# Attention products in a fused attention and two-MLP kernel: three rounded products replaced by one fp32 product, with the two heads on separate parts of the array

## The chip, the cores and the metric

The kernel runs on 1 core of a Trainium2 chip. The metric is the device time of one execution, in microseconds (us). The kernel before takes 2152.38 us, the median of 3 runs (2146.97 to 2156.15). TensorE (PE in the profile) multiplies matrices, VectorE is DVE, ScalarE is ACT, GpSimd is POOL, and SyncE (SP) issues nearly all DMAs. PEld is the weight load of TensorE, which can lie beside the product before it.

## The reference

Three stages follow each other. Causal attention with a window of 128 and a linear position bias, for 4 batches, 8 heads, 576 positions and a head width of 64:

```
scores = q @ k.T / sqrt(64)
scores = where(0 <= rel < 128, scores - slope[h] * |rel|, -1e9)
attn   = softmax(scores)                 # sums get + 1e-9
x      = (attn @ v), heads side by side  # 2304 x 512, fp32
```

Then an MLP, `x = relu(x @ w_in)**2 @ w_out`, with w_in of 512 x 2048 and w_out of 2048 x 512. Then a soft mixture of 8 experts: gates from `x @ w_gate`, normalised 8 times over experts and tokens, and `sum over e of P[:, e] * (relu(x @ w1[e]) @ w2[e])`.

## The kernel before, in words

**Number formats.** TensorE takes two 32-bit formats here. In F32R a product is one pass, but its operands must have been rounded; to keep accuracy an operand is split into a rounded part (hi) and what is left (lo), and one product becomes three: hi·hi, hi·lo, lo·hi. The MLP and the experts are done in this way throughout (`mm3`, lines 119 to 121). In plain F32 nothing is split, and the trace shows each product as two PE instructions.

**Units of attention.** One unit is a batch, a pair of heads and either the first 384 query positions (three tiles of 128, here called a first unit) or the remaining 192 (a tile of 128 and one of 64; a rest unit). There are 32 units, 16 of each kind, in the order: the first units of batch 0 (4 pairs of heads), the rest units of batch 0, then batch 1, and so on. The two heads of a pair lie in the two halves of the partitions for q and k (64 rows each).

**Two ways of doing a unit.** The first `WHOLE_UNITS = 12` units (8 first units, 4 rest units) are done in plain F32: q is padded with zeros, so that a head's scores are a product over all 128 rows (lines 340 to 348), and the bias is added by a product with the identity. The other 20 units (8 first, 12 rest) are split: q, k, v and the softmax weights p each have a hi and a lo tile. Their scores (lines 352 to 354) are three products per head over that head's 64 rows; the bias is added on DVE (line 357).

**Values.** For all units, `block` (lines 396 to 410) multiplies v by the transposed weights. v lies with a block of 64 zero columns between its two heads, so that each head's product fills 128 columns and both heads add into the same 128 output partitions. A whole unit does one F32 product per head and block, a split unit three F32R products. A first unit does block 0 in the step of tile 1 and blocks 1 and 2 in the step of tile 2; a rest unit does blocks 3, 2 and 4 in one step (line 431).

**Where p and v come from.** p is transposed on TensorE into PSUM (line 392), copied by ACT (line 306 whole, line 114 split) and in a split unit subtracted by DVE (line 115). v of a whole unit is loaded straight into place when its scores are done (lines 279 to 285); v of a split unit is loaded with q and k two units ahead (line 205), then split by ACT and POOL (lines 290, 291).

**Order.** Attention is not a stage of its own. `plan` lists its steps (q: transpose q and k; s: scores; t: transpose p, then values), and `part` (called after parts of the MLP's steps) lets the attention steps of the next chunk of tokens run among the MLP products of the present one. Up to the start of the experts a scheduler orders the instructions of each engine; all that follows is in the order written. The attention products lie between 0 and 577 us of the span. PSUM banks of attention come from a pool of three (`ps_at`).

Of the kernel before, what the change touches and what calls it, by code (L numbers as in the profile page):

```python
# [29 lines left out]
def attention_moe_moe2(  # L30
# [12 lines left out]
    nc = tc.nc  # L43
# [125 lines left out]

    qtail, qwhole, vwhole, vsplit = [], [], [], []  # L170
    for i in range(SETS):

        qtail.append([ap.tile([P, 2, TAIL], F32R, name=f"qtail{i}{n}") for n in range(2)])
        qwhole.append(ap.tile([P, 7 * P], F32, name=f"qwhole{i}"))
        nc.gpsimd.memset(qwhole[i], 0.0)
        vwhole.append(ap.tile([P, 3, 3, D], F32, name=f"vwhole{i}"))
        nc.gpsimd.memset(vwhole[i][:, :, 1, :], 0.0)
        vsplit.append([ap.tile([P, 3, 3, D], F32R, name=f"vsplit{i}{n}") for n in range(2)])
        for n in range(2):
            nc.vector.tensor_scalar_mul(  # L180
                vsplit[i][n][:, :, 1, :], ones[:, None, :D].to_broadcast([P, 3, D]), 0.0
            )
    def tails_ready():

        for i in range(SETS):
            for n in range(2):
                nc.scalar.activation(qtail[i][n].rearrange("p j c -> p (j c)"), ones, AF.Copy, scale=0.0)
        for hp in range(NPAIR):
            for j in range(2):
                nc.scalar.copy(  # L190
                    tbias[j * TAIL : (j + 1) * TAIL, hp, :], raw(bias[0:TAIL, 2 * hp + j, : P + TAIL])
                )

    def attention_load(n, b, hp, rest):

        h0 = 2 * hp
        t = {"rest": rest, "alone": b == 0 and not rest, "whole": n < WHOLE_UNITS}
        for nm, src in (("k", k), ("q", q), ("v", v)):
            if nm == "v" and t["whole"]:
                continue  # L200
            r = t[nm] = ap.tile([P, 3, 2, D], F32, name=f"{nm}raw", tag=f"{nm}raw", bufs=2)
            r0 = 0 if not rest else EARLY - (0 if nm == "q" else P)
            r1 = FULL * P if rest else EARLY
            for j in range(2):
                nc.sync.dma_start(
                    r[:, : (r1 - r0) // P, j, :], src[b, h0 + j, r0:r1, :].rearrange("(t p) d -> p t d", p=P)
                )
            if rest:
                nc.sync.dma_start(
                    r[:TAIL, (r1 - r0) // P], src[b, h0 : h0 + 2, r1:, :].rearrange("j p d -> p j d")  # L210
                )
        return t

    def attention_qk(n, t):

        rest = t["rest"]
        hi, lo = {}, {}
        for nm in "k" if t["whole"] else "kq":
            hi[nm] = ap.tile([P, EARLY], F32R, name=f"{nm}h", tag=f"{nm}h", bufs=2)
            t[nm + "h"] = hi[nm]  # L220
            if not t["whole"]:
                lo[nm] = t[nm + "l"] = ap.tile([P, EARLY], F32R, name=f"{nm}l", tag=f"{nm}l", bufs=2)

        def put_whole(pk, pq):
            nc.scalar.copy(raw(hi["k"][:, : pk.shape[-1]]), pk)
            qw = t["qw"] = qwhole[n % SETS]
# [9 lines left out]
        def turn(ps, nm, blocks, tail):  # L236
# [7 lines left out]
            return ps[:, :o]  # L244

        if not rest:
            pk = turn(at_ps("tp_k", t), "k", 3, 0)
            if not t["whole"]:
                split_ps(pk, hi["k"], lo["k"])
            pq = turn(at_ps("tp_q", t), "q", 3, 0)  # L250
            if t["whole"]:
                put_whole(pk, pq)
            else:
                split_q(pq, hi["q"], lo["q"])
        else:
            both = at_ps("tp", t)
            w = 2 * P + TAIL
            pk = turn(both, "k", 2, 1)
            if not t["whole"]:
                split_ps(pk, hi["k"][:, :w], lo["k"][:, :w])  # L260
            pq = turn(both[:, w:], "q", 1, 1)
            if t["whole"]:
                put_whole(pk, pq)
                return
            split_q(pq[:, :P], hi["q"][:, :P], lo["q"][:, :P])
            t["qt"] = qtail[n % SETS]
            for j in range(2):
                r = slice(j * D, (j + 1) * D)
                split_q(pq[r, P:], *[x[r, j, :] for x in t["qt"]])

    def attention_v(n, t):

        rest = t["rest"]
        if t["whole"]:
            vh, = t["vs"] = [vwhole[n % SETS]]
            b, hp, _ = units[n]
            for j in range(2):
                src = v[b, 2 * hp + j]
                if rest:
                    nc.sync.dma_start(  # L280
                        vh[:, :2, 2 * j], src[2 * P : FULL * P].rearrange("(t p) d -> p t d", p=P)
                    )
                    nc.sync.dma_start(vh[:TAIL, 2, 2 * j], src[FULL * P :])
                else:
                    nc.sync.dma_start(vh[:, :, 2 * j], src[:EARLY].rearrange("(t p) d -> p t d", p=P))
            return
        vh, vl = t["vs"] = vsplit[n % SETS]
        cuts = [(slice(0, P), slice(0, 2)), (slice(0, TAIL), slice(2, 3))] if rest else [(slice(0, P), slice(0, 3))]
        for rows, ts in cuts:
            nc.scalar.activation(vh[rows, ts, ::2], t["v"][rows, ts], AF.Copy)  # L290
            nc.gpsimd.tensor_sub(vl[rows, ts, ::2], t["v"][rows, ts], raw(vh[rows, ts, ::2]))

    def split_q(ps, hi, lo):
        nc.scalar.activation(hi, ps, AF.Copy, scale=-(D ** -0.5))
        nc.vector.scalar_tensor_tensor(lo, ps, -(D ** -0.5), raw(hi), op0=ALU.mult, op1=ALU.subtract)

    def weights(t):
        return [
            ap.tile([P, 2, 6 * P], F32R, name=f"p{n}", tag=f"p{n}", bufs=2) for n in range(1 if t["whole"] else 2)
        ]  # L300

    def put_p(t, pv, rows, at):
        w = pv.shape[-1]
        dst = [x[:rows, :, at : at + w] for x in t["p"]]
        if t["whole"]:
            nc.scalar.copy(raw(dst[0]), pv)
        else:
            split_ps(pv, *dst)

    def attention_scores(hp, t, i):  # L310
# [16 lines left out]
        z = ap.tile([P, 2], F32, name="z", tag="z", bufs=3)  # L327
        ops = []
        for j in range(0 if t["whole"] else heads):
            r = slice(0, P) if tail else slice(j * D, (j + 1) * D)  # L330
            if tail:
                qh, ql = [x.rearrange("p j c -> p (j c)") for x in t["qt"]]
            else:
                qh, ql = [t[n][r, (i - qb0) * P : (i - qb0 + 1) * P] for n in ("qh", "ql")]
            kh, kl = [t[n][r, k0 : k0 + nk] for n in ("kh", "kl")]
            ops.append(((qh, kh), (qh, kl), (ql, kh)))
        if t["whole"]:
# [6 lines left out]
            for j, sc in enumerate(scs):  # L344
                q0 = 6 * P if tail else (2 * (i - qb0) + j) * P
                nc.tensor.matmul(
                    sc, lhsT=t["qw"][:, q0 : q0 + P], rhs=raw(t["kh"][:, k0 : k0 + nk]), start=False, stop=j == heads - 1,
                    skip_group_check=True,
                )
            nc.vector.tensor_reduce(out=m[:, :heads], in_=sv, op=ALU.min, axis=AX.X)  # L350
        else:
            for x in range(3):
                for sc, (lhs, rhs) in zip(scs, [o[x] for o in ops]):
                    nc.tensor.matmul(sc[:, :nk], lhsT=lhs, rhs=rhs, start=x == 0, stop=x == 2)  # L354
        for j, sc in enumerate(scs if not t["whole"] else ()):
# [18 lines left out]
    def attention_weights(t, i):  # L374
# [3 lines left out]
        if not t["p"]:  # L378
            t["p"] = weights(t)
        kb0 = 2 if t["rest"] else 0  # L380
        at = max(0, 2 * (i - kb0) - 1) * P
        pt = at_ps("pt", t)
        if tail:
            for kb in range(2):
                nc.tensor.transpose(pt[:, kb * P : (kb + 1) * P], s[:, 0, kb * P : (kb + 1) * P], ident)
            for kb, rows in ((0, P), (1, TAIL)):
                put_p(t, pt[:rows, kb * P : (kb + 1) * P].rearrange("p (j c) -> p j c", j=2), rows, at + kb * P)
            return
        pv = pt[:, : 2 * blocks * P].rearrange("p (j c) -> p j c", j=2)
        for j in range(2):  # L390
            for kb in range(blocks):
                nc.tensor.transpose(pv[:, j, kb * P : (kb + 1) * P], s[:, j, kb * P : (kb + 1) * P], ident)  # L392
        put_p(t, pv, P, at)

    def block(t, kb, dst, a, w, first, last):

        rows = TAIL if kb == FULL else P
        kb -= 2 if t["rest"] else 0
        vs = [x[:rows, kb].rearrange("p a d -> p (a d)") for x in t["vs"]]
        a += 2 * kb * P  # L400
        n, ops = 0, 1 if t["whole"] else 3
        for j in range(2):
            ls = [x[:, j * D : j * D + P] for x in vs]
            rs = [x[:rows, j, a : a + w] for x in t["p"]]
            for l, r in ((0, 0), (0, 1), (1, 0))[:ops]:
                l, r = (ls[0], raw(rs[0])) if t["whole"] else (ls[l], rs[r])
                nc.tensor.matmul(  # L407
                    dst, lhsT=l, rhs=r, start=first and n == 0, stop=last and n == 2 * ops - 1, skip_group_check=True
                )
                n += 1  # L410

# [925 lines left out]
```

## Time and profile before

| | |
|---|---|
| median of 3 runs | 2152.38 us |
| the profiled execution | 2151.79 us, span 2150.0 us |
| TensorE busy | 2087.5 us, 97% of the span |
| weight loads busy | 1915.1 us, 89% |
| DVE / ACT / POOL busy | 68% / 46% / 49% |
| granted TensorE clock, mean | 0.992 |
| the chain that ended last | PE 79%, DVE 10%, ACT 3%, DMA 3% |

A busy TensorE isn't one at its peak: the recorded length of a product holds its way through the array, and neighbours overlap. What a product costs is read from the distance of starts: from the start of a product before a group to the start of the second product behind it, less the usual distances of those products. The first product behind a group often starts by the record before its weights are there, so its own start isn't taken.

### The profile page before, as it was taken

What the parts mean: (1) busy time and instruction counts of PE and PEld (TensorE: products, weight loads), DVE (VectorE), ACT (ScalarE), POOL (GpSimd) and SP (SyncE); (2) the same over time, 40 slices, a digit from 0 to 9 for tenths busy, and PEclk for the clock granted to TensorE, in tenths of its full rate; (3) what the DMA queues carried; (4) which work ended last, traced back from release to release, by engine and by line L of the source; (5) the groups of instructions that cost most, each with busy time, mean ns of one, the idle gap of its engine ahead of it and who ended that gap; (6) DMA issues with size and microseconds to landing.
All of it is one profiled execution on the core that took longest, in us unless ns stands there. A gap on an engine that the chain in (4) does not pass through costs nothing.

```text
span 2150.0 us, 32105 instructions
## 1 busy us (share of the span) xinstructions
PE 2087.5 (97%) x11260; PEld 1915.1 (89%) x11260; DVE 1463.2 (68%) x2480; ACT 981.2 (46%) x1982; POOL 1054.7 (49%) x697
## 2 busy tenths in 40 slices
PE   6999999999999999999999999999999999999998
PEld 5887777777798788899998999999999999999998
DVE  7996444442425888887778567776678667777766
ACT  7775444443324444444444444444444444444343
POOL 1113223222246778888888445544447344554442
PEclk9999999999999999999999999999999999999999
DMA  7787546455574877798888977787877877778773
GB/s 211 233 248 243 154 135 176 134 157 167 199 243 168 313 272 289 281 333 293 309 300 305 333 261 255 249 271 260 258 259 266 267 257 257 258 244 275 260 260 125
DMA packets 281792, 525.46 MB, mean 244 GB/s; under 512 B 85648, under 2 KB 129824, under 8 KB 277536
## 3 DMA queue, kind: packets, MB, share of 16 engines
q1 hardware_dynamic: 281632, 523.42, 72.3%
q8 instruction: 90, 1.47, 0.3%
q14 instruction: 70, 0.57, 0.1%
HBM read 379.60 MB, written 143.73 MB: 243 GB/s over the span
## 4 chain that ended last, share of the span: by engine, by line
PE 79%; DVE 10%; ACT 3%; DMA 3%; issue 2%; POOL 1%; SPq 1%; ACTq 0%; POOLq 0%; DVEq 0%
PE y L120 9%; PE y L119 9%; PE y L121 9%; PE g L119 9%; PE g L121 9%; PE g L120 9%; PE xo L407 3%; PE h L119 3%; PE h L120 3%; PE h L121 3%; PE acc L119 3%; PE acc L121 3%; PE acc L120 2%; PE sc L354 1%; PE pt L392 1%
## 5 line engine op out<-in xcount | busy, mean ns | idle before, releaser
L1157 POOL TENSOR_TENSOR rb<-R,rb 128x768 fp32r<-128x768 f32 x95 | 210.8, 2220 | 337.6 <-ACT rb L1152 329.8
L1188 DVE TENSOR_TENSOR a<-y,a 128x384 f32<-128x384 f32 x434 | 239.8, 553 | 179.7 <-PE y L121 177.6
L1157 POOL TENSOR_TENSOR rt<-R,rt 128x768 fp32r<-128x768 f32 x125 | 238.9, 1923 | 146.4 <-issue 61.7
L111 POOL TENSOR_TENSOR gl<-r,gh 128x512 fp32r<-128x512 f32 (+1 forms) x80 | 99.3, 1242 | 403.9 <-ACT gh L110 388.9
L111 POOL TENSOR_TENSOR w2a<-r,w2a 128x1024 fp32r<-128x1024 f32 x64 | 155.0, 2422 | 66.7 <-ACT w2a L110 66.7
L1152 ACT ACTIVATE rt<-R 128x768 fp32r<-128x768 f32 x128 | 107.7, 842 | 148.0 <-DVE R L1139 89.6
L119 PE MATMUL g<-xt,w1o 128*128 128x384 f32 x512 | 172.9, 338 | 0.9 <-ACT u L880 0.6
L121 PE MATMUL g<-xt,w1o 128*128 128x384 f32 x512 | 172.5, 337 | 0.0
L119 PE MATMUL y<-rt,w2o 128*128 128x384 f32 x512 | 172.3, 336 | 0.2
L120 PE MATMUL g<-xt,w1o 128*128 128x384 f32 x512 | 172.3, 336 | 0.0
L121 PE MATMUL y<-rt,w2o 128*128 128x384 f32 x512 | 172.1, 336 | 0.0
L120 PE MATMUL y<-rt,w2o 128*128 128x384 f32 x512 | 171.8, 336 | 0.0
L119 PE MATMUL y<-w2a,rh 128*128 128x512 f32 x384 | 151.2, 394 | 0.0
L120 PE MATMUL y<-w2a,rh 128*128 128x512 f32 x384 | 150.8, 393 | 0.2 <-POOL w2a L111 0.2
L121 PE MATMUL y<-w2a,rl 128*128 128x512 f32 x384 | 150.1, 391 | 0.0
L1134 DVE TENSOR_TENSOR R<-R,pb 128x768 f32<-128x768 f32 x128 | 139.0, 1087 | 5.3 <-ACT R L1247 3.0
L769 DVE SCALAR_TENSOR_TENSOR r<-h,r 128x512 f32<-128x512 f32 (+1 forms) x80 | 50.9, 636 | 134.4 <-ACT r L767 134.3
L119 PE MATMUL y<-rb,w2o 128*128 128x384 f32 x384 | 130.3, 339 | 2.8 <-DVE a L1188 2.1
L120 PE MATMUL y<-rb,w2o 128*128 128x384 f32 x384 | 130.1, 339 | 2.4 <-POOL rb L1157 2.4
L121 PE MATMUL y<-rb,w2o 128*128 128x384 f32 x384 | 129.9, 338 | 0.0
L119 PE MATMUL g<-xb,w1o 128*128 128x384 f32 x384 | 129.1, 336 | 0.0
L121 PE MATMUL g<-xb,w1o 128*128 128x384 f32 x384 | 129.1, 336 | 0.0
(252 smaller groups left out, 6105.9 us busy)
## 6 DMA issues: line engine op xcount, KB each, us to landing
w1o<-d_w SPq DMA_DIRECT2D x448, 256.0 KB, 3.0
w2o<-d_w SPq DMA_DIRECT2D x224, 512.0 KB, 4.0
d_w<-w1a SPq DMA_DIRECT2D x32, 1792.0 KB, 11.5
d_w<-w2a SPq DMA_DIRECT2D x32, 1536.0 KB, 8.0
a<-d_in SPq DMA_DIRECT2D x64, 512.0 KB, 3.8
b<-d_out SPq DMA_DIRECT2D x64, 512.0 KB, 3.7
r<-in_moe_w_dram SPq DMA_DIRECT2D x64, 512.0 KB, 4.3
u<-in_moe_w_in_dram SPq DMA_DIRECT2D x16, 512.0 KB, 4.7
```

Source lines behind the costliest of these rows:

```text
L111: (eng or nc.gpsimd).tensor_sub(lo, src, raw(hi))
L119: nc.tensor.matmul(ps, lhsT=lh, rhs=rh, start=first, stop=False, **kw)
L120: nc.tensor.matmul(ps, lhsT=lh, rhs=rl, start=False, stop=False, **kw)
L121: nc.tensor.matmul(ps, lhsT=ll, rhs=rh, start=False, stop=last, **kw)
L354: nc.tensor.matmul(sc[:, :nk], lhsT=lhs, rhs=rhs, start=x == 0, stop=x == 2)
L392: nc.tensor.transpose(pv[:, j, kb * P : (kb + 1) * P], s[:, j, kb * P : (kb + 1) * P], ident)
L407: nc.tensor.matmul(dst, lhsT=l, rhs=r, start=first and n == 0, stop=last and n == 2 * ops - 1, skip_group_check=True)
L769: nc.vector.scalar_tensor_tensor(g[:, :n], ph[:, :n], 0.0, r[:, :n], op0=ALU.max, op1=ALU.mult)
L1134: nc.vector.tensor_mul(r, r, pb[:, None, :].to_broadcast([P, 2, HALF]))
L1152: nc.scalar.activation(x[:, 0], R[m, f, h], AF.Copy)
L1157: eng.tensor_sub(x[:, 1], R[m, f, h], raw(x[:, 0]))
L1188: nc.vector.tensor_add(acc[dst][:, dt], ps[:, :HALF], acc[dst][:, dt])
```

## The change

Split units are done in plain F32 too, but without the zero padding of the whole ones: k and q are copied once each (`kf`, `qf`), and each head's scores are one F32 product over its 64 rows. v has no zero columns any more; for all 32 units each head's product has 64 columns and writes the half of the output partitions that belongs to that head. The tiles of hi and lo parts for q, k, v and p go, and with them the splits on ACT, DVE and POOL. v of every unit is now loaded in the way of the whole units, after its scores. The tail tiles of q are zeroed by POOL instead of ACT.

```diff
-        for nm, src in (("k", k), ("q", q), ("v", v)):
-            if nm == "v" and t["whole"]:
-                continue
+        for nm, src in (("k", k), ("q", q)):
...
+        def put_k(pk):
+            nc.scalar.copy(kf[:, : pk.shape[-1]], pk)
...
+        if t["whole"]:
+            put_whole(pq)
+        else:
+            n0 = P if rest else EARLY
+            nc.vector.tensor_scalar_mul(t["qf"][:, :n0], pq[:, :n0], -(D ** -0.5))
...
-            nc.scalar.activation(vh[rows, ts, ::2], t["v"][rows, ts], AF.Copy)
-            nc.gpsimd.tensor_sub(vl[rows, ts, ::2], t["v"][rows, ts], raw(vh[rows, ts, ::2]))
+        vw = t["v"] = ap.tile([P, 3, 2, D], F32, name="v", tag="v", bufs=2)
+        b, hp, _ = units[n]
+        for j in range(2):
+            src = v[b, 2 * hp + j]
+            if rest:
+                nc.sync.dma_start(vw[:, :2, j], src[2 * P : FULL * P].rearrange("(t p) d -> p t d", p=P))
+                nc.sync.dma_start(vw[:TAIL, 2, j], src[FULL * P :])
+            else:
+                nc.sync.dma_start(vw[:, :, j], src[:EARLY].rearrange("(t p) d -> p t d", p=P))
...
-            for x in range(3):
-                for sc, (lhs, rhs) in zip(scs, [o[x] for o in ops]):
-                    nc.tensor.matmul(sc[:, :nk], lhsT=lhs, rhs=rhs, start=x == 0, stop=x == 2)
+            for j, sc in enumerate(scs):
+                r = slice(0, P) if tail else slice(j * D, (j + 1) * D)
+                lhs = t["qt"].rearrange("p j c -> p (j c)") if tail else t["qf"][r, (i - qb0) * P : (i - qb0 + 1) * P]
+                nc.tensor.matmul(sc[:, :nk], lhsT=lhs, rhs=t["kf"][r, k0 : k0 + nk], start=True, stop=True)
...
-        put_p(t, pv, P, at)
+        nc.scalar.copy(t["p"][:, :, at : at + blocks * P], pv)
...
-        n, ops = 0, 1 if t["whole"] else 3
         for j in range(2):
-            ls = [x[:, j * D : j * D + P] for x in vs]
-            rs = [x[:rows, j, a : a + w] for x in t["p"]]
-            for l, r in ((0, 0), (0, 1), (1, 0))[:ops]:
-                l, r = (ls[0], raw(rs[0])) if t["whole"] else (ls[l], rs[r])
-                nc.tensor.matmul(
-                    dst, lhsT=l, rhs=r, start=first and n == 0, stop=last and n == 2 * ops - 1, skip_group_check=True
-                )
-                n += 1
+            nc.tensor.matmul(
+                dst[j * D : (j + 1) * D], lhsT=t["v"][:rows, kb, j], rhs=t["p"][:rows, j, a : a + w],
+                start=first, stop=last, skip_group_check=True,
+            )
```

How the order of instructions on TensorE changes is shown at three places. An F32 product is one row here and two instructions in the trace; the last figures of a row are partitions and columns of the output.

First place: the scores of one tile of a rest unit (the second unit that isn't whole), among products of the MLP (`h`, `acc`) and transposes (`pt`). Before:

```order
L119 MATMUL h_2365<-xh_91,a 128x512
L120 MATMUL h_2365<-xl_92,a 128x512
L121 MATMUL h_2365<-xh_91,a 128x512
L354 MATMUL sc<-kh,qh 128x256 x2
L354 MATMUL sc<-kl,qh 128x256 x2
L354 MATMUL sc<-kh,ql 128x256 x2
L385 MATMUL pt<-ident,s 128x128 x2
```

After:

```order
L120 MATMUL h_2343<-xl_92,a 128x512
L121 MATMUL h_2343<-xh_91,a 128x512
L345 MATMUL pt<-ident,s 128x128 x4
L304 MATMUL sc<-kf,qf 128x256 x2
L335 MATMUL pt<-ident,s 128x128
L119 MATMUL h_2422<-xh_91,a 128x512
```

Six products, in which the heads alternate, have become two, one head after the other.

Second place: the values of the first rest unit that isn't whole (`p_2444` and `vsplit_175` are the hi parts, `p_2445` and `vsplit_176` the lo parts), cut after 9 of 18 products. Before:

```order
L121 MATMUL h_2457<-xh_91,a 128x512
L407 MATMUL xo<-p_2444,vsplit_175 128x192
L407 MATMUL xo<-p_2445,vsplit_175 128x192
L407 MATMUL xo<-p_2444,vsplit_176 128x192
L407 MATMUL xo<-p_2444,vsplit_175 128x192
L407 MATMUL xo<-p_2445,vsplit_175 128x192
L407 MATMUL xo<-p_2444,vsplit_176 128x192
L407 MATMUL xo<-p_2444,vsplit_175 128x128
L407 MATMUL xo<-p_2445,vsplit_175 128x128
L407 MATMUL xo<-p_2444,vsplit_176 128x128
```

After, all of the unit's values:

```order
L119 MATMUL acc_2584<-gh,b 128x512
L354 MATMUL xo<-p,v 64x192 x2
L354 MATMUL xo<-p,v 64x128 x2
L354 MATMUL xo<-p,v 64x64 x2
L537 MATMUL lt<-xh_89,wgs 72x384 x4
```

18 products of 128 output partitions have become 6 of 64.

Third place: a whole first unit of batch 1, block 0 of the values and the next unit's scores. Before:

```order
L119 MATMUL acc_981<-gh,b 128x384
L407 MATMUL xo<-p_1762,vwhole_183 128x256 x2
L340 MATMUL sc<-bias,ident_r 128x256
L346 MATMUL sc<-kh,qwhole_171 128x128 x2
L392 MATMUL pt<-ident,s 128x128 x2
```

After:

```order
L121 MATMUL acc_990<-gh,b 128x384
L354 MATMUL xo<-p,v 64x256
L289 MATMUL sc<-bias,ident_r 128x256
L295 MATMUL sc<-kf,qwhole_170 128x128
L354 MATMUL xo<-p,v 64x256
L295 MATMUL sc<-kf,qwhole_170 128x128
L119 MATMUL h_1977<-xh_89,a 128x384
```

The two heads of a block no longer follow each other here: the scheduler has put score products of another unit between them.

## Rows read from the trace of the kernel before

**Rows 1.** Busy time by stretch: us, engines (instructions), granted clock, DMA share, GB/s.

```profile
0.00:54.00 54.00, 36.09 (x165) 27.55 (x166) 42.13 (x120) 38.20 (x109) 9.33 (x28) 0.91 0.72 211
54.00:577.00 523.00, 514.01 (x2735) 412.85 (x2734) 282.47 (x824) 262.21 (x701) 120.50 (x124) 1.00 0.59 182
```

**Rows 2.** Waits of PE from 180 to 577 us: total, times, longest.

```profile
PE xo L407 <- DVE p L115: 3.3, 6, 0.8
```

**Rows 3.** Groups by line: DVE's part of the split of p.

```profile
L115 DVE TENSOR_TENSOR p<-pt,p 128x512 fp32r<-128x512 f32 x28 | 19.2, 685 | 6.1 <-ACT p L114 5.9
```

**Rows 4.** Timeline of PE (start, length): split scores, one tile, both heads.

```profile
216.22 0.40 PE L121 MATMUL acc<-gh,b 128*128 128x512 f32 x1
...
216.77 0.28 PE L354 MATMUL sc<-kl,qh 64*128 64x256 f32 x2
216.89 0.28 PE L354 MATMUL sc<-kh,ql 64*128 64x256 f32 x2
...
217.44 0.39 PE L120 MATMUL acc<-gl,b 128*128 128x512 f32 x1
```

**Rows 5.** Timeline of PE: F32 scores of a whole unit, two heads.

```profile
163.35 1.02 PE L346 MATMUL sc<-kh,qwhole 128*128 128x256 f32 x4
164.21 0.27 PE L392 MATMUL pt<-ident,s 128*128 128x128 f32 x1
```

**Rows 6.** Timeline of PE: split scores of a tail tile.

```profile
226.00 0.39 PE L121 MATMUL acc<-gh,b 128*128 128x512 f32 x1
226.23 0.25 PE L354 MATMUL sc<-kh,qtail 128*128 128x192 f32 x1
...
226.55 0.41 PE L119 MATMUL acc<-gh,b 128*128 128x512 f32 x1
```

**Rows 7.** Timeline of PE: values of a split rest unit, 1 and 17 products.

```profile
219.05 0.40 PE L120 MATMUL h<-xl,a 128*128 128x512 f32 x1
219.35 0.36 PE L407 MATMUL xo<-p,vsplit 128*128 128x192 f32 x1
...
219.80 0.40 PE L119 MATMUL h<-xh,a 128*128 128x512 f32 x1
220.08 2.22 PE L407 MATMUL xo<-p,vsplit 128*128 128x192 f32 x17
...
222.57 0.40 PE L121 MATMUL h<-xh,a 128*128 128x512 f32 x1
```

**Rows 8.** Timeline of PE: values of split first units, 1 and 11 products.

```profile
252.03 0.39 PE L119 MATMUL acc<-gh,b 128*128 128x512 f32 x1
252.29 0.39 PE L407 MATMUL xo<-p,vsplit 128*128 128x256 f32 x1
...
252.74 0.39 PE L121 MATMUL acc<-gh,b 128*128 128x512 f32 x1
...
258.08 1.47 PE L407 MATMUL xo<-p,vsplit 128*128 128x256 f32 x11
...
259.67 0.40 PE L120 MATMUL h<-xl,a 128*128 128x512 f32 x1
```

**Rows 9.** Timeline of PE: F32 values of a whole first unit, blocks 1 and 2.

```profile
178.74 1.47 PE L407 MATMUL xo<-p,vwhole 128*128 128x256 f32 x8
180.05 0.47 PE L240 MATMUL tp<-ident,qraw 128*128 128x128 f32 x2
```

**Rows 10.** Timeline of PE: F32 values of a whole rest unit.

```profile
80.82 0.34 PE L120 MATMUL h<-xl,a 128*128 128x384 f32 x1
81.03 1.95 PE L407 MATMUL xo<-p,vwhole 128*128 128x192 f32 x12
...
83.19 0.33 PE L119 MATMUL h<-xh,a 128*128 128x384 f32 x1
83.36 0.34 PE L120 MATMUL h<-xl,a 128*128 128x384 f32 x1
```

**Rows 11.** Instructions on the whole units' v: landing of its DMAs.

```profile
DMA to landing us min/median/max: 1.8/3.8/6.4
```

More of the change, by code (lines that the diff above doesn't have):

```diff
@@ L168, in at_ps @@
         return pool.tile([P, 512], F32, name=name, tag=tag)
-    qtail, qwhole, vwhole, vsplit = [], [], [], []
+    qtail, qwhole = [], []
     for i in range(SETS):
-        qtail.append([ap.tile([P, 2, TAIL], F32R, name=f"qtail{i}{n}") for n in range(2)])
+        qtail.append(ap.tile([P, 2, TAIL], F32, name=f"qtail{i}"))
         qwhole.append(ap.tile([P, 7 * P], F32, name=f"qwhole{i}"))
         nc.gpsimd.memset(qwhole[i], 0.0)
[L176 to L181, printed above, removed]
-            )
     def tails_ready():
         for i in range(SETS):
-            for n in range(2):
-                nc.scalar.activation(qtail[i][n].rearrange("p j c -> p (j c)"), ones, AF.Copy, scale=0.0)
+            nc.gpsimd.memset(qtail[i], 0.0)
         for hp in range(NPAIR):
@@ L216, in attention_qk, with put_whole @@
         rest = t["rest"]
[L217 to L225, printed above, removed]
+        kf = t["kf"] = ap.tile([P, EARLY], F32, name="kf", tag="kf", bufs=2)
+        if not t["whole"]:
+            t["qf"] = ap.tile([P, EARLY], F32, name="qf", tag="qf", bufs=2)
+        def put_whole(pq):
             qw = t["qw"] = qwhole[n % SETS]
@@ L244, in turn @@
             return ps[:, :o]
+        def put_k(pk):
+            nc.scalar.copy(kf[:, : pk.shape[-1]], pk)
         if not rest:
-            pk = turn(at_ps("tp_k", t), "k", 3, 0)
-            if not t["whole"]:
-                split_ps(pk, hi["k"], lo["k"])
+            put_k(turn(at_ps("tp_k", t), "k", 3, 0))
             pq = turn(at_ps("tp_q", t), "q", 3, 0)
[L251 to L254, printed above, removed]
         else:
@@ L257, in attention_qk @@
             w = 2 * P + TAIL
-            pk = turn(both, "k", 2, 1)
-            if not t["whole"]:
-                split_ps(pk, hi["k"][:, :w], lo["k"][:, :w])
+            put_k(turn(both, "k", 2, 1))
             pq = turn(both[:, w:], "q", 1, 1)
[L262 to L269, printed above, removed]
+        if t["whole"]:
[4 more added lines that the diff above has]
+            if rest:
+                qt = t["qt"] = qtail[n % SETS]
+                for j in range(2):
+                    r = slice(j * D, (j + 1) * D)
+                    nc.vector.tensor_scalar_mul(qt[r, j, :], pq[r, P:], -(D ** -0.5))
@@ L271, in attention_v @@
     def attention_v(n, t):
         rest = t["rest"]
[L274 to L286, printed above, removed]
@@ L287, in attention_v @@
-        vh, vl = t["vs"] = vsplit[n % SETS]
-        cuts = [(slice(0, P), slice(0, 2)), (slice(0, TAIL), slice(2, 3))] if rest else [(slice(0, P), slice(0, 3))]
-        for rows, ts in cuts:
-            nc.scalar.activation(vh[rows, ts, ::2], t["v"][rows, ts], AF.Copy)
-            nc.gpsimd.tensor_sub(vl[rows, ts, ::2], t["v"][rows, ts], raw(vh[rows, ts, ::2]))
-    def split_q(ps, hi, lo):
-        nc.scalar.activation(hi, ps, AF.Copy, scale=-(D ** -0.5))
-        nc.vector.scalar_tensor_tensor(lo, ps, -(D ** -0.5), raw(hi), op0=ALU.mult, op1=ALU.subtract)
@@ L297, in weights @@
[L297 to L308, printed above, removed]
+        vw = t["v"] = ap.tile([P, 3, 2, D], F32, name="v", tag="v", bufs=2)
+        b, hp, _ = units[n]
@@ L310, in attention_scores @@
+        for j in range(2):
+            src = v[b, 2 * hp + j]
+            if rest:
+                nc.sync.dma_start(vw[:, :2, j], src[2 * P : FULL * P].rearrange("(t p) d -> p t d", p=P))
+                nc.sync.dma_start(vw[:TAIL, 2, j], src[FULL * P :])
+            else:
+                nc.sync.dma_start(vw[:, :, j], src[:EARLY].rearrange("(t p) d -> p t d", p=P))
     def attention_scores(hp, t, i):
@@ L327, in attention_scores @@
         z = ap.tile([P, 2], F32, name="z", tag="z", bufs=3)
[L328 to L336, printed above, removed]
         if t["whole"]:
@@ L346, in attention_scores @@
                 nc.tensor.matmul(
-                    sc, lhsT=t["qw"][:, q0 : q0 + P], rhs=raw(t["kh"][:, k0 : k0 + nk]), start=False, stop=j == heads - 1,
+                    sc, lhsT=t["qw"][:, q0 : q0 + P], rhs=t["kf"][:, k0 : k0 + nk], start=False, stop=j == heads - 1,
                     skip_group_check=True,
@@ L378, in attention_weights @@
         if not t["p"]:
-            t["p"] = weights(t)
+            t["p"] = ap.tile([P, 2, 6 * P], F32, name="p", tag="p", bufs=2)
         kb0 = 2 if t["rest"] else 0
@@ L386, in attention_weights @@
             for kb, rows in ((0, P), (1, TAIL)):
-                put_p(t, pt[:rows, kb * P : (kb + 1) * P].rearrange("p (j c) -> p j c", j=2), rows, at + kb * P)
+                c = at + kb * P
+                nc.scalar.copy(
+                    t["p"][:rows, :, c : c + TAIL], pt[:rows, kb * P : (kb + 1) * P].rearrange("p (j c) -> p j c", j=2)
+                )
             return
@@ L398, in block @@
         kb -= 2 if t["rest"] else 0
-        vs = [x[:rows, kb].rearrange("p a d -> p (a d)") for x in t["vs"]]
         a += 2 * kb * P
-        n, ops = 0, 1 if t["whole"] else 3
         for j in range(2):
-            ls = [x[:, j * D : j * D + P] for x in vs]
-            rs = [x[:rows, j, a : a + w] for x in t["p"]]
-            for l, r in ((0, 0), (0, 1), (1, 0))[:ops]:
-                l, r = (ls[0], raw(rs[0])) if t["whole"] else (ls[l], rs[r])
-                nc.tensor.matmul(
-                    dst, lhsT=l, rhs=r, start=first and n == 0, stop=last and n == 2 * ops - 1, skip_group_check=True
-                )
-                n += 1
+            nc.tensor.matmul(
+                dst[j * D : (j + 1) * D], lhsT=t["v"][:rows, kb, j], rhs=t["p"][:rows, j, a : a + w],
+                start=first, stop=last, skip_group_check=True,
+            )
     def put_x(ps, hp, t0, n):
```

## The prediction

> **What bounds the kernel now.** I read busy time by stretch first, then PE's waits in the stretch of the change, then the timeline of PE there. From 54 to 577 us, where nearly all attention products lie, PE is busy 514 of 523 us at the full clock (2.4 GHz), while DVE is busy 282, ACT 262 and POOL 120 us and the DMAs 59% [rows 1]. So a microsecond of PE saved there is one off the end, and work taken from DVE, ACT and POOL gives next to nothing by itself. Before 54 us PE is busy only 36 of 54 us; four of the 32 units have their values near there, and part of what I count for them may be hidden. What is left of waiting is small: from 180 to 577 us PE waits 3.3 us for DVE's part of p [rows 2]. The question is thus what PE's time in attention becomes.
>
> **What a product costs on PE.** Four facts come from the timeline.
> A split score group has six products, but the records come in pairs: both heads start together, 0.12 us after the pair before (216.77, 216.89) [rows 4]. So two heads on separate 64 rows of the array run side by side in F32R. The whole group takes 217.44 − 216.22 less two usual distances of 0.23 (226.00 to 226.23 [rows 6]), that is 0.76 us. Three slots of 0.12 explain 0.36; the other 0.40 I put on the two changes between 128-row and 64-row use, 0.20 each, since the tail tile, which uses all 128 rows, has no such remainder: three products in 0.32 us [rows 6].
> The Trainium skill, TensorEngine Tiling (Array Packing), Key Properties, says that changing the tiling mode drains TensorE. The 0.40 us agree for rows; that it holds for columns too no row here shows. By the rule the sum is the one below; without it for columns it would be some 21 us less (third rival).
> An F32 product is two passes. Four passes of 256 columns take 0.86 us (163.35 to 164.21), 0.215 each [rows 5], nearly twice an F32R one. Four of 256 and four of 128 take 1.31 (178.74 to 180.05), so one of 128 takes 0.11 [rows 9]; 192 columns I put at 0.16 in proportion.
> Nothing in the trace shows two heads on separate columns, nor F32 passes side by side. From one side they cost the full number of passes; from the other, since starts stay in order (head 0 twice, then head 1 twice), a pair's four passes take three slots, and a longer run half its passes plus one. I take the overlap, the nearest row being the F32R pairs of rows 4, and keep the other end for the range.
>
> **Part by part** (PE time; counts from the loops: 8 first and 12 rest units leave the split form, 8 first and 4 rest were whole).
> 1. Scores of 256 columns, 8 × 2 + 12 = 28 groups: 0.76 before, 3 × 0.215 + 0.40 = 1.05 after: +0.29 each, +8.0 us. Without overlap 4 × 0.215 + 0.40 = 1.26: +14.0.
> 2. Scores of 128 columns, 8 groups: three slots of 0.11 either way: 0 (without overlap +0.11 each, +0.9). Tail scores, 12: three products in 0.32 [rows 6] against two passes of 0.16: 0.
> 3. Values of split rest units, 12. Before: the one that goes ahead 219.80 − 219.05 − 0.46 = 0.29, the other 17 222.57 − 219.80 − 0.46 = 2.31, together 2.60 [rows 7]. After: four passes of 0.16 and four of 0.11, 1.08, paired 0.54 + 0.16 = 0.70; four passes of 64 columns and 64 rows, for which I take 0.06 (between 0.05, in proportion to columns, and 0.11, where a full weight load sets the pace), paired 0.18; three changes of array use (into columns, to 64 rows, back) 0.60. Sum 1.48: −1.12 each, −13.4 us. Without overlap 1.92: −8.2.
> 4. Values of split first units, 8. Before: one ahead 252.74 − 252.03 − 0.46 = 0.25, eleven 259.67 − 258.08 − 0.23 = 1.36 [rows 8], 0.124 each, so 0.25 + 5 × 0.124 = 0.87 for block 0 and 1.61 for blocks 1 and 2: 2.48. After: 3 × 0.215 + 0.40 = 1.05 and 0.65 + 0.215 + 0.40 = 1.26: 2.31. −0.17 each, −1.4 us. Without overlap 1.26 + 1.70 = 2.96: +3.8.
> 5. Values of whole first units, 8. Before 0.86 + 1.31 = 2.17 without any change of array use [rows 5, 9]; after 2.31: +1.1 us, without overlap +6.3. In the new order the columns are entered 53 times, where 32 + 16 = 48 groups would need 48; each of the five more (the third place shows one) costs two changes, 0.40: +2.0.
> 6. Values of whole rest units, 4: before 83.36 − 80.82 less three usual distances of 0.17 = 2.03 [rows 10], after 1.48: −2.2 us, without overlap 1.92, −0.4.
> 7. Waits: p is now ready after ACT's copy; the DVE half of 0.685 us [rows 3] goes, and with it the 3.3 us of rows 2. Late next is ACT's copy itself, on which the whole units wait already.
> 8. Work off PE: the splits of q, k, v and p on DVE, ACT and POOL go and q's copy stays with DVE. Their cover is PE's 514 of 523 us: nothing. The POOL memsets and ACT copies of the start swap places; PE waits there for others: nothing.
> 9. Loads of v come after the scores instead of two units ahead, with 12 more DMAs. Landing takes 3.8 us, at most 6.4 [rows 11], and one step of attention is followed by several MLP products, so PE's own work covers it; the whole units do the same, and no wait of PE names v's load. Nothing, or, if the cover failed, up to 3.8 us for each of 20 units.
> Sum: 8.0 − 13.4 − 1.4 + 1.1 + 2.0 − 2.2 − 3.3 = −9.2 us. The profiled execution took 2151.79 us, 0.6 below the median of 2152.38; 2151.8 − 9.2 = 2142.6, which I give as 2143 us. The large gain on the rest units' values is half eaten by slower scores and by changes of array use: 204 in the order before, 276 after.
>
> **The rivals.**
> *Columns do not overlap, rows do.* For it: no row shows it. Against: the row pairs of rows 4. Sum: 8.0 − 8.2 + 3.8 + 6.3 + 2.0 − 0.4 − 3.3 = +8.2: 2160 us.
> The Trainium skill, TensorE: Matmul & The Clock Gate, Part 3, gives 2.38 times for three small column tiles side by side, which speaks against this rival; no run here shows it.
> *F32 passes never overlap* (the other side). The mechanism: each of the two passes keeps the array to itself, so that scores cost 0.50 and 0.11 more per group as well: 8.2 + 6.0 + 0.9 = +15.1: 2167 us, slower. For it: every F32 product in the trace uses all 128 rows and columns, so none could have paired. It decides once the second head's passes start only at the end of the first's; with scores alone unpaired it is near 2149.
> *A change to columns costs nothing.* Then 53 entries at 0.40 go: −9.2 − 21.2 = −30.4: 2121 us; half of it, 2132. Against: changes to 64 rows do cost 0.20 each way.
>
> **How the numbers follow.** The forecast 0.58, columns unpaired 0.20, nothing paired 0.12, free column changes (whole or half) 0.10. A measurement here tells about 0.5% from no change, some 10.8 us, so below 2141.6 is faster and above 2163.1 slower. The forecast's own range is 2136 to 2149, as the change into columns is 0.1 to 0.25 and the scheduler's new order is worth a few us: about 0.4 of it lies below 2141.6. Faster: 0.23 + 0.10 = about 0.34. Slower: 0.85 of the unpaired case, 0.3 of the columns case, about 0.16. Within: 0.50. The range that holds 8 in 10 reaches from half-free changes, 2131, into the unpaired case, 2164.
>
> **What would show it.** In the new timeline the score passes of the two heads should start as 1, then 2 together, then 1, at 0.215 us, and a group with its changes take 1.05 us; values of a rest unit 1.5 us instead of 2.60, of a first unit 2.3. PE should name no wait for DVE's p, and none for v's DMA. The stretch behind 577 us should keep its length of 1573 us, give or take a few. It is wrong if second heads start only after the first's two passes, if the empty time around 64-column groups isn't near 0.2 us a side, or if the time moves in the experts.

## The result, and the profile after

The changed kernel takes 2118.85 us (2117.58 to 2119.06), the kernel before 2151.89 us (2146.97 to 2156.15), four runs each: a ratio of 0.9846 [0.9824, 0.9868], or 33 us. I forecast 2143 us with 2131 as the low end. The sign of the likeliest case was right, the size and the range were not.

Busy time by stretch comes first, with the columns of [rows 1], for the changed kernel:

```profile
0.00:54.00 54.00, 34.42 (x182) 24.00 (x183) 41.40 (x118) 38.56 (x108) 9.24 (x29) 0.91 0.72 212
54.00:577.00 523.00, 511.13 (x2654) 389.48 (x2655) 271.52 (x765) 253.83 (x649) 117.04 (x105) 1.00 0.63 197
577.00:2117.00 1540.00, 1506.59 (x8223) 1446.36 (x8221) 1117.41 (x1515) 666.00 (x1147) 906.44 (x531) 0.99 0.77 267
```

PE is still the bound between 54 and 577 us (511 of 523 busy, full clock, 2.4 GHz), but the stretch now holds work that came later before. The markers say where the time went: the last values product starts at 544.4 us instead of 575.2, the first expert product at 623.5 instead of 656.0 (32.5 earlier), and what follows the last values product takes 1572.6 us instead of 1574.8. So the gain was made in the attention stage. There the stretches of PE between two MLP products that hold score or values products last 106.5 us instead of 137.1 (summed over the whole trace, each from the start of the MLP product ahead to the start of the one behind, less the usual distance).

Waits of PE from 180 to 577 us of the changed kernel, all that are named (total, times, longest):

```profile
PE lt L537 <- ACT xh L114: 2.1, 2, 2.0
PE h L119 <- DMA a<-d_in: 1.3, 1, 1.3
PE lt L542 <- DVE xl L115: 0.5, 1, 0.5
PE pt L335 <- DMA kraw<-in_k_dram: 0.2, 1, 0.2
```

The wait of [rows 2] is gone, and no other wait for p takes its place in this stretch. The later loads of v do no harm: landing takes up to 7.2 us, against 6.4 in [rows 11], but among the instructions on v's tile PE waits for them only 0.3 us in the whole run.

```profile
DMA to landing us min/median/max: 1.8/2.9/7.2
```

Now the products, on the timeline of PE (start, length). Scores of one pair of heads, answering [rows 4]; the second fence cuts the view off at 200.38 us, so that its count says how many passes had begun by then:

```profile
199.74 0.40 PE L121 MATMUL acc<-gh,b 128*128 128x512 f32 x1
200.07 0.70 PE L304 MATMUL sc<-kf,qf 64*128 64x256 f32 x4
200.70 0.50 PE L119 MATMUL h<-xh,a 128*128 128x512 f32 x1
201.04 0.40 PE L120 MATMUL h<-xl,a 128*128 128x512 f32 x1
```

```profile
200.07 0.49 PE L304 MATMUL sc<-kf,qf 64*128 64x256 f32 x2
```

By 200.38 two passes had begun, both by 200.08; they are one of each head, for two passes of one head start 0.2 us apart, as the run with one head after the other shows below. The other two follow together. The group costs 201.04 − 199.74 − 2 × 0.23 = 0.84 us (0.83 in the mean over all), against my 1.05. Values of a first unit, block 0 and then blocks 1 and 2, answering [rows 8, 9]:

```profile
245.47 0.39 PE L119 MATMUL acc<-gh,b 128*128 128x512 f32 x1
245.79 0.65 PE L354 MATMUL xo<-p,v 128*64 128x256 f32 x4
246.37 0.50 PE L120 MATMUL acc<-gl,b 128*128 128x512 f32 x1
246.71 0.40 PE L121 MATMUL acc<-gh,b 128*128 128x512 f32 x1
...
250.11 0.39 PE L119 MATMUL h<-xh,a 128*128 128x512 f32 x1
250.42 0.87 PE L354 MATMUL xo<-p,v 128*64 128x256 f32 x8
251.22 0.50 PE L120 MATMUL h<-xl,a 128*128 128x512 f32 x1
251.56 0.40 PE L121 MATMUL h<-xh,a 128*128 128x512 f32 x1
```

They cost 246.71 − 245.47 − 0.46 = 0.78 and 251.56 − 250.11 − 0.46 = 0.99 us, against 1.05 and 1.26. Values of a rest unit, answering [rows 7, 10]:

```profile
204.28 0.40 PE L121 MATMUL acc<-gh,b 128*128 128x512 f32 x1
204.65 1.02 PE L354 MATMUL xo<-p,v 128*64 128x192 f32 x12
205.61 0.50 PE L119 MATMUL acc<-gh,b 128*128 128x512 f32 x1
205.94 0.40 PE L120 MATMUL acc<-gl,b 128*128 128x512 f32 x1
```

That is 205.94 − 204.28 − 0.46 = 1.20 us (1.16 in the median), against 1.48 forecast and 2.60 before. Two heads on separate columns do run side by side, and in these groups the forecast was too dear by 0.22 to 0.32 us: about one slot of a pass, 0.21, and in the values somewhat cheaper changes of array use.

The change of array use can be read in the same rows. Between full-array products the usual distance is 0.23 us. From the last of them to the first column product it is 245.79 − 245.47 = 0.32, and from the first product after the columns to the next 246.71 − 246.37 = 0.34: some 0.1 us more on either side. In between, 246.37 − 245.79 = 0.58 us hold 2 × 0.215 of passes and another 0.15. So of the 0.78 us, 0.43 are passes; the 0.35 left over I count as the two changes, where I had put 0.40. The rule of the Trainium skill, TensorEngine Tiling (Array Packing), Key Properties, that a change of tiling mode drains TensorE, agrees with the trace for columns too, with these 0.35 us.

### The profile page after: what moved, and what is told of

It is laid out like the page before. It is cut to its first block, busy times and chain, and to the rows that moved or that the text cites. A ratio compares the mean times of both kernels' runs of the same rounds, so it can differ in the third digit from the quotient of the medians.

```text
span 2117.0 us, 31449 instructions
## 1 busy us (share of the span) xinstructions
PE 2052.1 (97%) x11056; PEld 1859.8 (88%) x11056; DVE 1430.3 (68%) x2396; ACT 958.4 (45%) x1902; POOL 1032.7 (49%) x665
## 4 chain that ended last, share of the span: by engine, by line
PE 59%; DVE 9%; ACT 2%; issue 2%; DMA 1%; POOL 1%; SPq 0%; ACTq 0%; DVEq 0%; POOLq 0%
PE y L120 9%; PE y L121 9%; PE y L119 9%; PE g L119 9%; PE g L121 9%; PE g L120 9%; DVE rl L954 1%; DVE o L922 1%; ACT rh L953 1%; DMA d_w<-w2a 1%; DVE o L920 1%; DVE s L644 1%; DVE s L642 1%; PE acc L120 1%; PE acc L121 1%
```

## The experiments

Each is an edit of the changed kernel, and its number is compared with that kernel's 2118.85 us. Run again on another chip, it took 2119.37 us (2118.26 to 2121.07), 0.9853 [0.9834, 0.9873] of before:

> The changed kernel once more, beside the next run on the same chip. 2119 us if what was measured holds: the ratio 0.985 with at most 0.002 either way.

**Columns taken away: v padded again, F32 kept.**

```diff
...
-                dst[j * D : (j + 1) * D], lhsT=t["v"][:rows, kb, j], rhs=t["p"][:rows, j, a : a + w],
-                start=first, stop=last, skip_group_check=True,
+                dst, lhsT=t["v"][:rows, kb].rearrange("p a d -> p (a d)")[:, j * D : j * D + P],
+                rhs=t["p"][:rows, j, a : a + w],
+                start=first and j == 0, stop=last and j == 1, skip_group_check=True,
```

> The changed kernel with one part undone: v has its zero columns again, so that each head's value product (still one F32 product, all units) fills 128 columns, and no columns are used apart. Theory A (the gain is TensorE time, because the two heads' F32 passes run fully side by side on separate columns): a first unit's values go back to 2.17 us from 0.78 + 0.99 = 1.77, a rest unit's to 2.03 from 1.16, over 16 units each: +6.4 + 13.9 = +20 us, 2139 us. Theory B (the gain beyond the forecast comes from the shorter way of p, without DVE, and from the lighter DVE, ACT and POOL): these stay as they are, so within 6 us of the changed kernel's 2118.9.

2133.02 us (2132.76 to 2136.94), 0.9917 [0.9902, 0.9931] of before: 14 us slower than the changed kernel. The rest unit's group on the timeline of PE:

```profile
206.22 0.40 PE L121 MATMUL acc<-gh,b 128*128 128x512 f32 x1
206.59 1.95 PE L356 MATMUL xo<-p,vwhole 128*128 128x192 f32 x12
208.47 0.51 PE L119 MATMUL acc<-gh,b 128*128 128x512 f32 x1
208.81 0.40 PE L120 MATMUL acc<-gl,b 128*128 128x512 f32 x1
```

It costs 208.81 − 206.22 − 0.46 = 2.13 us (2.04 in the median), as in [rows 10], and a first unit's two groups 0.95 + 1.33. So separate columns are worth 14 of the 33 us. The other 19 go, by subtraction, with one F32 product in place of three and what hangs on it; of them the way of p without DVE is some 8 (below), and no run takes the rest apart. By groups alone the columns should be worth 16 × (2.28 − 1.77) + 16 × (2.04 − 1.16) = 22; that four first units lie in the opening, where PE isn't the bound, and that in five units of the changed kernel the heads of some pairs don't stand together, may account for the difference, but no run separates this.

**Rows taken away: q padded for all units, scores on 128 rows.**

```diff
...
-                lhs = t["qt"].rearrange("p j c -> p (j c)") if tail else t["qf"][r, (i - qb0) * P : (i - qb0 + 1) * P]
-                nc.tensor.matmul(sc[:, :nk], lhsT=lhs, rhs=t["kf"][r, k0 : k0 + nk], start=True, stop=True)
+                q0 = 6 * P if tail else (2 * (i - qb0) + j) * P
+                nc.tensor.matmul(
+                    sc[:, :nk], lhsT=t["qw"][:, q0 : q0 + P], rhs=t["kf"][:, k0 : k0 + nk], start=True, stop=True
+                )
```

> The changed kernel with the other part undone: the later units' q is padded with zeros as in the whole units, so that a head's F32 score product takes all 128 rows and no rows are used apart. Theory A, from measured groups: a pair of 256 columns needs 4 x 0.215 = 0.86 us without any change of array use, against 0.83 with the heads side by side and two changes (+0.03, 28 groups), a pair of 128 columns 0.44 against 0.62 (8 groups): -0.6 us in all, 2118 us; so separate rows give back in changes what they save in passes. Rival (separate rows save the half of the passes that they save on paper): +0.43 each for 28 and +0.2 for 8 groups, +13.6 us, 2132 us.

2119.81 us (2118.1 to 2121.89), 0.9853 [0.9837, 0.987]: no different from the changed kernel.

```profile
199.08 0.39 PE L121 MATMUL acc<-gh,b 128*128 128x512 f32 x1
199.31 1.02 PE L292 MATMUL sc<-kf,qwhole 128*128 128x256 f32 x4
199.98 0.58 PE L119 MATMUL h<-xh,a 128*128 128x512 f32 x1
200.40 0.40 PE L120 MATMUL h<-xl,a 128*128 128x512 f32 x1
```

Here no gap stands ahead of the group (199.31 − 199.08 = 0.23), and four passes one after the other cost 200.40 − 199.08 − 0.46 = 0.86 us. On separate rows it is two slots and two changes, 0.83. What the heads save side by side, the changes take back; with 128 columns the padded form is even cheaper (0.44 to 0.62). Separate rows for scores are no part of the gain.

**The order of starts: all blocks of head 0, then all of head 1.**

```diff
...
-            block(t, 1, xo[:, P : 3 * P], 0, 2 * P, False, False)
-            block(t, 2, xo[:, 2 * P : 3 * P], 0, P, False, True)
+            for j in range(2):
+                block(t, 1, xo[:, P : 3 * P], 0, 2 * P, False, False, [j])
+                block(t, 2, xo[:, 2 * P : 3 * P], 0, P, False, True, [j])
...
```

> The changed kernel with the value products of a step in another order: all blocks of head 0, then all of head 1, instead of the heads in turn. The same products on the same columns. Theory A1 (products start in the order written, and only those that stand next to each other as a pair, one per head, have their passes side by side): in the step of tile 2 of a first unit head 1 starts with the last pass of head 0, so the group goes from 0.99 to about 1.5 us, and a rest unit's from 1.16 to about 1.5 and two more changes of array use, 1.9: 16 x 0.5 + 16 x 0.7 = +19 us, 2138 us. Theory A2 (each half of the columns takes its products on its own, whatever stands between): first units stay at 0.99; rest units have two changes more, 0.34 each unit, +5 us, 2124 us.

2132.26 us (2130.76 to 2133.7), 0.9909 [0.9894, 0.9923]: 13 us slower, and instructive by where. A first unit, and then the same view cut off at 256.58 us:

```profile
256.01 0.39 PE L119 MATMUL h<-xh,a 128*128 128x512 f32 x1
256.32 0.88 PE L354 MATMUL xo<-p,v 128*64 128x256 f32 x8
257.13 0.50 PE L120 MATMUL h<-xl,a 128*128 128x512 f32 x1
257.47 0.40 PE L121 MATMUL h<-xh,a 128*128 128x512 f32 x1
```

```profile
256.32 0.44 PE L354 MATMUL xo<-p,v 128*64 128x256 f32 x2
```

It costs 1.00 us, as with the heads in turn, though each head's block 2 is now written ahead of the other head's block 1: two passes had begun by 256.58. A rest unit, and the view of it cut off at 209.56 us:

```profile
208.98 0.40 PE L121 MATMUL acc<-gh,b 128*128 128x512 f32 x1
209.36 1.96 PE L354 MATMUL xo<-p,v 128*64 128x192 f32 x12
211.24 0.50 PE L119 MATMUL acc<-gh,b 128*128 128x512 f32 x1
211.58 0.39 PE L120 MATMUL acc<-gl,b 128*128 128x512 f32 x1
```

```profile
209.36 0.38 PE L354 MATMUL xo<-p,v 128*64 128x192 f32 x1
```

Here one pass had begun, and the group costs 211.58 − 208.98 − 0.46 = 2.14 us (2.08 in the median): 16 × (2.08 − 1.16) = 14.7, near the slowdown of 13.4. Head 0's tail block uses 64 rows, and behind it head 1 has to change back to 128: with a change of array use between them the heads no longer meet. The rest unit also has two products between the heads where the first unit has one. But it isn't this distance: in the changed kernel one product of the full array stands between the two heads of a whole first unit, and they don't meet either:

```profile
123.64 0.65 PE L354 MATMUL xo<-p,v 128*64 128x256 f32 x2
124.22 0.38 PE L289 MATMUL sc<-bias,ident_r 128*128 128x256 f32 x1
124.53 0.65 PE L354 MATMUL xo<-p,v 128*64 128x256 f32 x2
125.11 0.71 PE L295 MATMUL sc<-kf,qwhole 128*128 128x128 f32 x4
```

Each head's two passes take 0.58 us to the next product's start, as long as the four passes of both heads together above (245.79 to 246.37). So it isn't the written order that decides, but whether the use of the array stays the same from one head's products to the other's. The Trainium skill, TensorE: Matmul & The Clock Gate, Part 3, says that products start strictly in program order; the first unit here starts in another order than the kernel writes. Whether TensorE, the compiler or the scheduler that orders the kernel's instructions put the products in turn is not settled by these runs.

**DVE put back on the path of p:** over ACT's copy it takes the larger of the copy and its source, which are equal, so that p is late as before.

```diff
...
+        if not t["whole"]:
+            pd = t["p"][:, :, at : at + blocks * P]
+            nc.vector.tensor_tensor(out=pd, in0=pv, in1=pd, op=ALU.max)
...
```

> The changed kernel with DVE put back into the way of p: after ACT's copy of the later units' p, DVE reads PSUM and the copy and writes the greater of the two (the same values) over it, an operation of the shape of the removed subtraction (0.685 us for 128x512, 60 of them). TensorE's work stays as it is. Theory A: at most the 3.3 us of waits that the kernel before had come back, 2119 to 2123 us. Theory B (the short way of p and the lighter DVE carry the surplus over the forecast, some 24 us): most of it goes, 2135 us or more.

2127.19 us (2123.75 to 2128.0), 0.9882 [0.9867, 0.9897]: 8.3 us slower, between the two expectations. Two waits of PE for p are new from 180 to 577 us, together 5.2 us:

```profile
PE xo L358 <- DVE p L341: 3.7, 5, 1.6
...
PE xo L358 <- DVE p L350: 1.5, 2, 0.8
```

The new order of instructions also puts values between the two heads of four score tiles, one of them here:

```profile
271.69 0.40 PE L121 MATMUL acc<-gh,b 128*128 128x512 f32 x1
272.02 0.70 PE L304 MATMUL sc<-kf,qf 64*128 64x256 f32 x2
272.65 0.87 PE L358 MATMUL xo<-p,v 128*64 128x256 f32 x8
273.45 0.70 PE L304 MATMUL sc<-kf,qf 64*128 64x256 f32 x2
274.07 0.50 PE L119 MATMUL acc<-gh,b 128*128 128x512 f32 x1
274.41 0.40 PE L120 MATMUL acc<-gl,b 128*128 128x512 f32 x1
```

It costs 274.41 − 271.69 − 0.46 = 2.26 us instead of 0.83 + 0.99, 1.8 us for four. The last 1.3 of the 8.3 us have no name.

**Scores alone as before:** q and k split, three F32R products, the values new.

```diff
...
+            for x, (ln, rn) in enumerate(((0, "kh"), (0, "kl"), (1, "kh"))):
+                for j, sc in enumerate(scs):
...
+                    nc.tensor.matmul(sc[:, :nk], lhsT=lhs, rhs=t[rn][r, k0 : k0 + nk], start=x == 0, stop=x == 2)
```

> One part of the change alone: values, v and p as in the changed kernel, but the later units' scores, q and k as before it (three F32R products per head on its 64 rows, hi and lo parts made on ACT and DVE). From groups measured before and after (0.76 against 0.83 us for a pair of 256 columns, 0.67 against 0.62 for one of 128, 0.32 against 0.33 for a tail): TensorE saves 28 x 0.07 - 8 x 0.05 = 1.6 us, so 2117 us if TensorE alone decides (theory A: the new form of the scores is no part of the gain). Rival: the splits of q and k on ACT and DVE were part of what held up TensorE, as the operation on p in the earlier run was (+8.3 for 60 operations); 20 splits of k and 32 of q would then cost some 5 us: 2124 us.

2121.13 us (2118.84 to 2123.08), 0.9863 [0.9842, 0.9885]. The score group is 0.75 us again, but the total can't be told from the changed kernel's, so this run decides between neither expectation. It does say that the values carry the gain: with the old scores nearly all of it is there.

**Two trials for a faster version.** The tail block over all 128 rows, with zeros in v's lower rows, so that the change to 64 rows goes; and only eight whole units instead of twelve.

```diff
+                nc.gpsimd.memset(vw[TAIL:, 2, j], 0.0)
...
-        rows = TAIL if kb == FULL else P
+        rows = P
```

> The changed kernel, with the last block of a rest unit's values done over all 128 rows (the lower 64 rows of v are set to zero by GpSimd, those of p are zero anyway) instead of 64 rows. Same passes; between the unit's value products the array use no longer changes (16 units). If a change costs 0.17 to 0.20 us as the groups say, a rest unit's group goes from 1.16 to 0.98 us: -2.9 us, 2116 us. Rival (a change among column uses is free, the 1.16 are passes): 2119 us, or more by the small operations on GpSimd.

```diff
-    WHOLE_UNITS = 12
+    WHOLE_UNITS = 8
```

> The changed kernel with 8 instead of 12 whole units: the first units of batch 1 get the form of the later units too (heads on separate rows, bias on DVE instead of a product with the identity). TensorE per unit: two tiles of 256 at 0.83 instead of 1.10, one of 128 at 0.62 against 0.56: -0.5 us, four units: -2 us, 2117 us, if TensorE decides. Rival: DVE, which is busy 114 of 126 us before 180 us, gets the bias additions (6 x 0.42 and 0.28 per unit against 3 reductions of 0.68) and TensorE waits for it: +2 us or more, 2121 us.

The first took 2118.21 us (2115.86 to 2120.84), 0.9852 [0.9833, 0.987]. A rest unit's group falls from 1.16 to 1.01 us in the median, so 16 × 0.15 = 2.4 us of PE go, which the total doesn't resolve. The second took 2121.48 us (2120.24 to 2124.24), 0.9868 [0.985, 0.9886], not faster. Its busy time by stretch, columns as in [rows 1]:

```profile
154.00:158.00 4.00, 1.66 (x13) 1.20 (x11) 4.00 (x15) 3.59 (x9) 0.00 (x0) 1.00 0.87 266
158.00:162.00 4.00, 3.33 (x16) 2.87 (x13) 4.00 (x9) 1.65 (x4) 1.43 (x1) 0.55 0.46 98
162.00:166.00 4.00, 4.00 (x15) 3.04 (x13) 1.39 (x6) 2.09 (x5) 0.00 (x0) 0.59 0.93 319
```

DVE is busy all of 154 to 162 us, PE 1.66 us of the first four, and then the granted clock is 0.55 and 0.59, near the lower level of 1.2 GHz, until 166. The longest wait of PE from 54 to 180 us falls there. It is not for DVE itself but for ACT's copy of p, and ACT is busy 3.59 of the first four us:

```profile
PE xo L354 <- ACT p L346: 2.3, 1, 2.3
```

So there PE is not the bound; that the bias on DVE makes the copy late isn't shown.

**The padded q and the 128-row tail together** need neither separate rows nor a change to 64 rows. They ran twice, on two chips.

> Both the padded q of the later units (no separate rows for scores, so no change of array use there) and the last block of values over 128 rows. If the two are independent, 2118.9 - 2.9 + 0 to 0.9 (what the padded q alone measured): 2116 to 2117 us, no better than the second alone. Rival (separate rows cost more than they give once other changes are gone): below 2115 us.

> The version with padded q and the last block over 128 rows once more, on the same chip as the changed kernel. From groups: 16 x 0.15 less for a rest unit's values (1.16 to 1.01), 28 x 0.03 more and 8 x 0.17 less for scores, together -2.9 us: 2116 us, if TensorE decides. If the earlier 2115.5 was the chip and not the kernel: 2119 us.

2115.51 us (2113.81 to 2116.49), 0.9838 [0.9821, 0.9855], and 2117.16 us (2115.74 to 2119.58), 0.9842 [0.9825, 0.9859]. It clearly beats the kernel before, and both medians lie 2 to 3 us under the changed kernel's, which the intervals of the ratios don't tell apart.

## Why the prediction was wrong

**What held.** PE bounds the stage; v's later loads are covered; the stage behind keeps its length. That the work taken from DVE, ACT and POOL brings nothing by itself fits the run with the splits of q and k put back (2121.13 us); for those of v, and for p beyond the wait on it, no run shows it. "A group with its changes" has them on rows and on columns, at 0.35 to 0.40 us where I took 0.40.

**The step that failed** is the one on how passes pair: "since starts stay in order (head 0 twice, then head 1 twice), a pair's four passes take three slots, and a longer run half its passes plus one". The rows show two and two together, and a longer run half its passes. I had taken the order of starts from the order in the code; the experiment with the heads one after the other shows that this order doesn't decide. The extra slot stood in every term that rests on pairs. By the medians measured in the changed kernel, with the counts of the prediction but for the entries, of which its trace has 56 and not 53:

| term | forecast, us | with measured groups, us |
|---|---|---|
| 1, scores of 256 columns | +8.0 | 28 × (0.83 − 0.76) = +2.0 |
| 2, scores of 128 columns | 0 | 8 × (0.62 − 0.67) = −0.4 |
| 3, split rest units | −13.4 | 12 × (1.16 − 2.60) = −17.3 |
| 4, split first units | −1.4 | 8 × (0.78 + 0.99 − 2.48) = −5.7 |
| 5, whole first units | +1.1 | 8 × (1.77 − 2.17) = −3.2 |
| 5, more entries | +2.0 | 8 × 0.35 = +2.8 |
| 6, whole rest units | −2.2 | 4 × (1.16 − 2.03) = −3.5 |
| 7, waits | −3.3 | −3.3, up to −8.3 |
| sum | −9.2 | −28.6, up to −33.6 |

The profiled executions differ by 2151.79 − 2118.78 = 33.0 us. Of the 24 us that I missed, the slot is 16: 28 × 0.215 for scores, 16 × 0.43 for the two groups of a first unit and 16 × (0.16 + 0.06) for a rest unit. Some 3 more are changes of array use that were cheaper than I took them, in the values above all, less the entries that I had missed. The last 4 lie outside the terms, and a little more than that, since the table doesn't hold what heads that are kept apart lose in overlap: 3 × 0.43 us for the first units, with some more for two rest units. **Term 7** was too small: the named wait of PE was 3.3 us, but putting DVE back on the path cost 8.3, with four broken pairs in it. The opening, which I counted at nothing, gave 2.5 us (the first MLP product starts at 53.8 instead of 56.3 us), some of it already in the whole units' terms; what it shares with them isn't separated.

**The rivals.** Unpaired columns (2160) and unpaired F32 passes (2167) are refuted by the rows. The free change to columns gave a number near the result, 2121, for a reason that is wrong: the change costs nearly what I took. That all passes pair without a remainder was missing as a rival, though in [rows 4] F32R pairs already stood together, two by two, with no odd one at either end. And the reading that every F32 product of the trace used all 128 rows was not exact: block 4 of the whole rest units has 64, with both heads on the same ones.

## What to carry to other kernels

Count side-by-side products by what the array holds, half the passes for two heads, and charge every change of array use, here 0.15 to 0.2 us; so long runs in one use pay, and a pair of short products does not. Keep what shares one use of the array together in the code: a 64-row block between the heads cost 13 us. And when a bound is taken as an ordering rule, look whether a row already shows that order; if not, its opposite belongs among the rivals.

## What was not expected of the hardware

F32 products of two heads overlap in full, on rows and on columns: four passes of 256 columns, 0.86 us one after the other, need two slots. The starts lie within 0.02 us of each other. And a group's two changes of array use are paid in parts, for columns about 0.1 us ahead of its first product, 0.15 us up to the next product of the full array and 0.1 us behind that one, which a view of busy time doesn't show, since PE counts as busy there.
